# A linear-attention block with an MLP: the output projection of two token blocks by seven block products

## The chip, the cores and the metric

The kernel runs on one core of a Trainium2 chip. The core has a matrix engine (PE; its weight loads are listed as PEld), a vector engine (DVE), a scalar engine (ACT), a general engine (POOL), and a queue that issues transfers (SP). They run side by side and wait for each other through semaphores. PE reads operands from the on-chip memory and writes into eight accumulator banks of 128 x 512 float32; In this kernel DVE and ACT read these banks, and POOL works on the on-chip memory alone. The metric is the time of one execution in microseconds; several executions give a median.

## The reference

The input x has 2048 tokens of 640 features. With xn = layernorm(x), the result is the sum of three parts:

```
q, k, v = split(xn @ wqkv)                 # 32 heads of 20
phi_q, phi_k = [softmax(p), softmax(-p)]   # p = q or k times a 20 x 20 matrix of the head
o = (phi_q (phi_k^T v)) / (phi_q sum(phi_k))
out = x + o @ wo + gelu(layernorm(xn) @ w1 + b1) @ w2 + b2
```

w1 is 640 x 1728, w2 is 1728 x 640, wo is 640 x 640. All is float32.

## The kernel before, in words

**Precision.** The kernel gives PE its operands in the format float32r. It splits each float32 operand exactly into a high part (ACT copies it into float32r) and a low part (DVE or POOL subtracts the high part). A product of two operands is three matmuls, high x high, high x low and low x high; the helper `mm3` (lines 69 to 72) issues them. The helper `split` is at lines 57 to 67: its copy is line 61, its subtraction line 64.

**Tiling.** Tokens stand in four blocks of 512, features in five chunks of 128 (KC = 5). The work of a block is turned: features on the partitions, tokens along the rows. `acc[b]` is the result of block b, five chunks of 128 x 512.

**Order.** The engines PE, DVE, ACT and POOL take their instructions in the order in which the program writes them; SP's order is chosen by the planner from its own estimate of when each transfer can go. The program's clock is the tick: each `mm3` calls `mlp.tick()`, which first runs the steps that are due (`mlp.after(n, step)` puts a step n ticks ahead) and then takes one step of a generator that runs beside (`mlp.beside`).

**Stages.** First the features of block 0, while the MLP begins. The generator `next_y` (from line 653) makes the features of block 1 beside the first two passes of the MLP: POOL subtracts the mean (line 679), DVE multiplies by the inverse deviation (681), ACT makes the high part (683), DVE the low part (685). It also ends what is left of the first block: gelu and split of its hidden units (lines 286 and 64), two tiles of second weights, and the last two instructions of the tokens' statistics, a reciprocal (161) and a product (162) that give `rs_all`, a factor which the attention features use later. Then follow blocks 0 and 1 of the MLP, the projections and the sums of the attention (line 905 and after), the MLP of blocks 2 and 3 beside the attention of all blocks, and the output projection.

**The output projection.** It starts at line 1407. For each block, output chunk m and feature chunk c, one `mm3` multiplies a 128 x 128 piece of wo by the attention output of the block, so that a column (one block and one m) is 15 matmuls into one bank; banks 6 and 7 take turns. DVE adds the bank to `acc[b][:, m]` (line 1423), and SP stores that (1424). The last column goes in two halves of 256 tokens. wo's high and low parts were loaded before (1295, 1297). The attention output of a block is made by `Attention`: `quotients` inverts the denominators (1246, stored by 1247), loads them spread over the partitions into `rx` (1251 to 1256), spreads them further with a shuffle on DVE (1262) and multiplies on POOL (1264). `Attention.split` makes the two parts of the operand, ACT at line 1283 and DVE at 1285, and for blocks 0 and 1 loads the MLP's result back (1289, tf<-a). The split of block 1 starts at tick 3 of the projection, of block 2 at tick 28, of block 3 at tick 53. In the same ticks the `quotients` of block 3 end: its shuffles and products stand at ticks 27 to 42.

The MLP of blocks 2 and 3 already uses, for its first weights, a scheme of seven block products in place of eight (`Mlp.cross`, `Mlp.sums`), with sums of weights made by POOL.

Of the kernel before, what the change touches and what calls it, by code (L numbers as in the profile page):

```python
# [8 lines left out]
F32 = mybir.dt.float32  # L9
F32R = mybir.dt.float32r  # L10
AF = mybir.ActivationFunctionType
ALU = mybir.AluOpType
# [3 lines left out]
P = 128  # L16
S, D, F, H, DH = 2048, 640, 1728, 32, 20
KC = D // P
NB = S // 512
# [27 lines left out]
def f(ap):  # L47
    return ap.bitcast(F32)
# [3 lines left out]
def tile_kernel(ctx: ExitStack, tc: tile.TileContext, x, xT, wkT, wqT, wv, wphi, wo, w1, b1, w2, b2,  # L52
                ident, mmask, emask, vsel, out):
    nc = tc.nc
# [14 lines left out]
    def mm3(ps, lh, ll, rh, rl, first, last, **kw):  # L69
        nc.tensor.matmul(ps, lh, rh, start=first, stop=False, **kw)  # L70
        nc.tensor.matmul(ps, lh, rl, start=False, stop=False, **kw)  # L71
        nc.tensor.matmul(ps, ll, rh, start=False, stop=last, **kw)  # L72
# [25 lines left out]
    acc = [None] * NB  # L98
# [4 lines left out]
    banks = ctx.enter_context(tc.tile_pool(name="banks", bufs=1, space=PSUM))  # L103
# [13 lines left out]
    rp = ys.enter_context(tc.tile_pool(name="raw", bufs=1))  # L117
    wp = ys.enter_context(tc.tile_pool(name="w", bufs=1))

    def mtile(i, dtype=F32):  # L120
        return mp.tile([P, 2, D if i < 5 else 512], dtype, name=f"m{i}")
    y = {}

    def load_x(ts, xp, tag="xb"):
        xbs = []
        for t in ts:
            xb = xp.tile([P, D], F32, name=tag)
            nc.sync.dma_start(xb, x[t * P:(t + 1) * P, :])
            xbs.append(xb)
        return xbs  # L130

    def stats(ts, xp, xbs, turned=False, eng=nc.vector):

        t0, n = ts[0], len(ts)
        st = xp.tile([P, n, 2, 6], F32, name="st", bufs=2)
        for i, (t, xb) in enumerate(zip(ts, xbs)):
            for h in range(2):
                nc.vector.bn_stats(st[:, i, h, :], xb[:, h * 320:(h + 1) * 320])  # L138
            nc.vector.bn_aggr(mv[:, t, :], st[:, i, :, :])
            yield  # L140


        ts = slice(t0, t0 + n)
        q = xp.tile([P, 2, n], F32, name="q", bufs=2)
        eng.tensor_scalar(q[:, 1, :], mv[:, ts, 1], 0.25 * (1 + EPS), 0.25 * EPS * EPS, op0=ALU.mult, op1=ALU.add)
        eng.tensor_scalar(q[:, 0, :], mv[:, ts, 1], 0.25, 0.25 * EPS, op0=ALU.mult, op1=ALU.add)
        yield

        sr = xp.tile([P, 2, n], F32, name="sr", bufs=2)
        rr = xp.tile([P, 2, n], F32, name="rr", bufs=2)  # L150
        nc.scalar.activation(sr, q, AF.Sqrt)
        nc.vector.reciprocal(rr, sr)
        nc.vector.tensor_tensor(rr, rr, q, op=ALU.mult)
        if turned:
            nc.vector.scalar_tensor_tensor(sr, sr, -1.0, rr, op0=ALU.mult, op1=ALU.subtract)
        else:
            nc.vector.tensor_tensor(sr, sr, rr, op=ALU.add)
        nc.vector.reciprocal(ry[:, ts], sr[:, 1, :])
        yield
        ra = xp.tile([P, n], F32, name="ra", bufs=2)  # L160
        nc.vector.reciprocal(ra, sr[:, 0, :])
        nc.vector.tensor_tensor(rs_all[:, ts], sr[:, 1, :], ra, op=ALU.mult)
# [41 lines left out]
    def load_rows(b, i=5):  # L204

        mr = mtile(i)
        loads[b] = nc.sync.dma_start(mr.rearrange("p a t -> p (a t)"),
                          (r_dram[1][0] if b == 1 else r_dram[2][b - 2]).rearrange("r t -> (r t)").unsqueeze(0).to_broadcast([P, 8 * P])).ins
        return mr
# [307 lines left out]
    mlp = Mlp((0, 1, 2, 3), ((0, 2), (1, 3)))  # L517

    def finish(p):
        for _ in p:  # L520
            pass
# [4 lines left out]
    x0 = load_x(range(2), xp)  # L526
    nc.sync.dma_start(idt, ident)
    wc, parts, dmas = {}, {}, {}
# [24 lines left out]
    x1 = load_x(range(4, 8), xp)  # L553
# [99 lines left out]
    def next_y():  # L653

        for _ in range(3):
            yield
        next(rows1)
        for z in zs[:2]:
            z()
        finish(rows1)  # L660
        mr = load_rows(1)
        first_raws.extend(raws(jobs[0]))
        for z in zs[2:]:
            z()
        for c in range(2, 4):
            parts[c][1]()
        for st in (s23, s47):
            step(st, 1)
        for _ in range(4):
            yield  # L670
        nc.vector.tensor_tensor(wpt[:, :, :, 1:], wpt[:, :, :, 1:], wpt[:, :, :, 0:1].to_broadcast([G6, 6, 6, DF]), op=ALU.subtract)
        for _ in range(9):
            yield
        xcs = {}
        for n in range(2 * KC + 5):
            c, i = divmod(n, 2)
            if i == 0 and c < KC:
                xcs[c] = xp.tile([P, D], F32, name="xb")[:, :512]
                nc.gpsimd.tensor_tensor(xcs[c], acc[1][:, c], mr[:, 0], op=ALU.subtract)
            if i == 0 and 0 <= (d := c - 1) < KC:  # L680
                nc.vector.tensor_tensor(xcs[d], xcs[d], mr[:, 1], op=ALU.mult)
            if i == 1 and 0 <= (d := c - 1) < KC:
                nc.scalar.activation(y[1][0][:, d], xcs[d], AF.Copy)
            if i == 0 and 0 <= (d := c - 2) < KC:
                nc.vector.tensor_tensor(y[1][1][:, d], xcs[d], f(y[1][0][:, d]), op=ALU.subtract)
            yield

    mlp.beside = next_y()
    p10 = mlp.passes(1, 0, [wc[2], wc[3]])
    next(p10)  # L690
# [191 lines left out]
    a = ExitStack()  # L882
# [129 lines left out]
    places = [acc01.tile([P, KC, 512], F32, name=f"acc{n}").rearrange("p c (j n) -> p (c j) n", n=P) for n in range(2)]  # L1012
    places = [p[:, j:j + 10] for p in places for j in (0, 10)] + [et.tile([P, 10, P], F32, name="et")]


    for t, i in [(t, i) for t in range(14) for i in range(4)] + TAIL:
        if (t, i) in ((4, 0), (8, 0)):
            b = t // 4 + 1
# [92 lines left out]
    t1 = sp.tile([VM, 5, 480], F32, name="t1")  # L1111
# [198 lines left out]
    wol, phs = [], []  # L1310
    ep = rx = None
# [20 lines left out]
    at = {}  # L1332
# [21 lines left out]
    ep = ctx.enter_context(tc.tile_pool(name="eB", bufs=1, side="right", reuse_waits="tile"))  # L1354
# [14 lines left out]
    for g in range(1, 6):  # L1369
        w2t, later = gathered(g)  # L1370
        hid, more = mlp.cross(g, (2, 3), before, later)
        if g < 5:
            parts = mlp.splits(g + 1)
        else:
            w1t, parts = mlp.take_pair(6, False, 1)
# [14 lines left out]
    w2t, parts = mlp.take_pair(6, True, 3)  # L1390
# [13 lines left out]
    finish(before)  # L1404
    load_ob(1)

    pw_ = Banks(6, 7)
    step = 0
    for b in range(NB):
        oh, ol = at[b].oh, at[b].ol  # L1410
        for m in range(KC):
            ms = slice(m * P, (m + 1) * P)

            for cols in [slice(0, 512)] if (b, m) != (NB - 1, KC - 1) else [slice(0, 256), slice(256, 512)]:
                pw = pw_()[:, cols]
                for c in range(KC):
                    mm3(pw, wol[0][c][:, ms], wol[1][c][:, ms], oh[:, c, cols], ol[:, c, cols], c == 0, c == KC - 1)
                    step += 1
                    mlp.tick()
                    for n, at_ in enumerate((3, 28, 53), 1):  # L1420
                        if step - at_ in range(KC + 1):
                            at[n].split(step - at_, nc.vector)
                nc.vector.tensor_tensor(acc[b][:, m, cols], pw, acc[b][:, m, cols], op=ALU.add)
                nc.sync.dma_start(out[ms, b * 512 + cols.start:b * 512 + cols.stop], acc[b][:, m, cols])


_INS = ["x", "xT", "wkT", "wqT", "wv", "wphi", "wo", "w1", "b1", "w2", "b2", "ident", "mmask", "emask", "vsel"]
# [60 lines left out]
```

## Time and profile before

| | us |
|---|---|
| median of 3 runs | 712.24 (711.95 to 714.44) |
| the profiled execution | 711.95 |
| its span, first to last instruction | 710.2 |
| PE busy | 703.4 |
| DVE busy | 514.5 |
| POOL busy | 421.7 |
| ACT busy | 341.5 |

The mean granted clock of PE is 0.999. In rows of a time line, the first number is the start in us from the span's start, the second the time in us (of all instructions of a row with a count), and what stands in brackets is how long the engine idled before and what ended that. In rows of waits the numbers are us in total, how often, and the longest. In rows of stretches the columns are PE, PEld, DVE, ACT and POOL busy with the count of instructions, the granted clock, the DMA engines' share and GB/s. A row's line can be that of a helper.

### The profile page before, as it was taken

How to read it: one execution, taken by the hardware profiler on the slowest of the kernel's cores; microseconds unless marked ns; L12 is line 12 of the kernel's file. 1: busy time of each engine (PE TensorE's matmuls, PEld its weight loads, DVE VectorE, ACT ScalarE, POOL GpSimd, SP SyncE). 2: the span in 40 equal slices, each digit the busy share in tenths (PEclk: the TensorE clock that was granted, in tenths of full speed). 3: DMA queues.
4: the chain of work that ended last, by engine and by line, in shares of the span. 5: the costliest groups of instructions: out<-in, count | busy, mean ns of one | idle time of the engine just before them, and what ended most of it. 6: DMA issues, size and time to landing. Idle time of an engine off the chain costs nothing.

```text
span 710.2 us, 9748 instructions
## 1 busy us (share of the span) xinstructions
PE 703.4 (99%) x3381; PEld 591.9 (83%) x3381; DVE 514.5 (72%) x819; ACT 341.5 (48%) x563; POOL 421.7 (59%) x362
## 2 busy tenths in 40 slices
PE   9999999999999999999999999999999999999998
PEld 7788888888888888888888888888888878888886
DVE  7977755978754788788888878757769686884622
ACT  6534554344334545544544547367666766450100
POOL 3621314577245997898787879458679887540400
PEclk9999999999999999999999999999999999999999
DMA  9823643485621227336401608963455568436222
GB/s 327 271 90 114 191 119 97 156 264 176 214 105 74 93 75 238 78 105 200 104 0 25 167 0 335 226 209 112 124 163 155 169 188 315 147 125 214 86 78 74
DMA packets 65767, 106.56 MB, mean 150 GB/s; under 512 B 7462, under 2 KB 31814, under 8 KB 63838
## 3 DMA queue, kind: packets, MB, share of 16 engines
q1 hardware_dynamic: 65414, 105.93, 46.7%
q8 instruction: 26, 0.43, 0.3%
q14 instruction: 23, 0.19, 0.1%
q10 hardware_dynamic: 304, 0.01, 0.0%
HBM read 71.37 MB, written 34.55 MB: 149 GB/s over the span
## 4 chain that ended last, share of the span: by engine, by line
PE 94%; DVE 3%; DMA 1%; ACT 1%; issue 0%; SPq 0%; DVEq 0%
PE bank L905 28%; PE bank L70 19%; PE bank L72 18%; PE bank L71 18%; PE bank L975 3%; PE bank L646 2%; PE bank L1213 1%; PE bank L1214 1%; DMA xb<-in_x 1%; DVE st L138 1%; DMA r<-sr 1%; PE bank L326 1%; PE bank L308 1%; PE bank L327 1%; PE bank L307 1%; PE bank L1145 1%
## 5 line engine op out<-in xcount | busy, mean ns | idle before, releaser
L905 PE MATMUL bank<-wkh,y 128*128 128x512 f32 (+1 forms) x480 | 139.5, 364 | 0.0
L70 PE MATMUL bank<-y,w 128*128 128x512 f32 (+1 forms) x294 | 114.3, 389 | 0.0
L71 PE MATMUL bank<-y,w 128*128 128x512 f32 (+1 forms) x294 | 113.7, 387 | 0.0
L72 PE MATMUL bank<-y,w 128*128 128x512 f32 (+1 forms) x294 | 113.6, 387 | 0.0
L64 POOL TENSOR_TENSOR w<-r,w 128x640 fp32r<-128x640 f32 x32 | 52.2, 1647 | 91.7 <-ACT w L61 62.2
L70 PE MATMUL bank<-m,w 128*128 128x512 f32 x260 | 102.4, 394 | 1.2 <-DVE acc L329 1.0
L72 PE MATMUL bank<-m,w 128*128 128x512 f32 x260 | 101.3, 390 | 0.0
L71 PE MATMUL bank<-m,w 128*128 128x512 f32 x260 | 101.2, 389 | 0.0
L905 PEld LDWEIGHTS bank<-wkh,y 128*128 128x128 f32 x480 | 87.5, 188 | 13.3
L905 PE MATMUL bank<-wkl,y 128*128 128x512 f32 (+1 forms) x240 | 87.4, 364 | 0.0
L70 PEld LDWEIGHTS bank<-y,w 128*128 128x128 f32 x294 | 55.2, 188 | 11.6 <-issue 0.4
L72 PEld LDWEIGHTS bank<-y,w 128*128 128x128 f32 x294 | 55.2, 188 | 11.3
L71 PEld LDWEIGHTS bank<-y,w 128*128 128x128 f32 x294 | 55.3, 188 | 11.0
L941 ACT ACTIVATE m<-m,rs_all 128x1280 f32<-128x1280 f32 x32 | 43.7, 1366 | 42.9 <-POOL m L940 42.8
L70 PEld LDWEIGHTS bank<-m,w 128*128 128x128 f32 x260 | 48.9, 188 | 12.1 <-DVE acc L329 1.5
L943 DVE TENSOR_REDUCE sm<-m 128x64 f32<-128x1280 f32 x32 | 47.4, 1482 | 14.9 <-ACT m L941 14.8
L905 PE MATMUL bank<-w,y 128*128 128x512 f32 x240 | 57.4, 391 | 0.0
L72 PEld LDWEIGHTS bank<-m,w 128*128 128x128 f32 x260 | 48.8, 188 | 10.3
L71 PEld LDWEIGHTS bank<-m,w 128*128 128x128 f32 x260 | 48.8, 188 | 9.9 <-DVE m L461 0.2
L940 POOL TENSOR_TENSOR m<-m,mx 128x640 f32<-128x640 f32 (+2 forms) x48 | 44.4, 938 | 19.3 <-DVE mx L929 19.3
L331 DVE TENSOR_TENSOR acc<-bank,acc 128x512 f32<-128x512 f32 x70 | 46.9, 683 | 10.9 <-PE bank L72 5.8
L905 PEld LDWEIGHTS bank<-w,y 128*128 128x128 f32 x240 | 44.4, 188 | 8.5
(186 smaller groups left out, 1447.2 us busy)
## 6 DMA issues: line engine op xcount, KB each, us to landing
r<-in_w SPq DMA_DIRECT2D x52, 320.0 KB
e<-e SPq DMA_DIRECT2D x40, 256.0 KB
e<-acc SPq DMA_DIRECT2D x52, 160.0 KB
acc<-in_xT SPq DMA_DIRECT2D x4, 1280.0 KB
t<-t SPq DMA_DIRECT2D x8, 512.0 KB
tf<-t SPq DMA_DIRECT2D x2, 1536.0 KB
xb<-in_x SPq DMA_DIRECT2D x8, 320.0 KB
t<-in_x SPq DMA_DIRECT2D x8, 320.0 KB
```

The costliest lines, as they stand in the source:

```text
L64: eng.tensor_tensor(lo, src, f(hi), op=ALU.subtract)
L70: nc.tensor.matmul(ps, lh, rh, start=first, stop=False, **kw)
L71: nc.tensor.matmul(ps, lh, rl, start=False, stop=False, **kw)
L72: nc.tensor.matmul(ps, ll, rh, start=False, stop=last, **kw)
L138: nc.vector.bn_stats(st[:, i, h, :], xb[:, h * 320:(h + 1) * 320])
L331: nc.vector.tensor_tensor(acc[b][:, m, :], pw, acc[b][:, m, :], op=ALU.add)
L646: nc.tensor.matmul(ps[:, u * nh * DF:(u + 1) * nh * DF], raw[:nh * DH, u * P:(u + 1) * P], wpt[:nh * DH, g, :nh, 1:], start=True, stop=True)
L905: nc.tensor.matmul(ps, lh[:, kc, c], rh[:, kc], start=n == 0, stop=n == 3 * KC - 1)
L940: subs[n, t] = nc.gpsimd.tensor_tensor(ep[:, s], a, b, op=ALU.subtract)
L941: exps[n, t] = nc.scalar.activation(e, e, AF.Exp, scale=rs_all[:, t:t + 1])
L943: nc.vector.tensor_reduce(sm, e.rearrange("p s (h f) -> p (s h) f", f=DH), axis=AX, op=ALU.add)
L975: nc.tensor.matmul(kvp[g // 2][:, (g % 2) * 240:(g % 2) * 240 + 240].rearrange("p (s f) -> p s f", s=4), v[:, g * VS:(g + 1) * VS], ft[:, ...
```

## The change

**Output projection.** Blocks 0 and 1 stay as they were, now by the function `column`. For blocks 2 and 3, four of the five output chunks and four of the five feature chunks are multiplied as 2 x 2 blocks of matrices with seven products in place of eight: with a_ij from wo and b_ij from the features (j is the token block, i the feature chunk in a pair), four sums s1 to s4 of wo and four differences t1 to t4 of the features are made first. The products run for k = 0, 1 (pairs of output chunks) and q = 0, 1 (pairs of feature chunks); a product's bank is read by DVE between two products, and goes on accumulating. The fifth feature chunk is added by `rest`, the fifth output chunk is a `column`. The sums of wo come from a new load of 512 x 512 numbers (`load_sums`, into the slot w3, which held the last second weights of the MLP); POOL adds (`add`), ACT makes the high parts into slot w1 (`hi_sum`), DVE the low parts into the slots of `kvs` and `s` (`lo_sum`). For the differences POOL subtracts (`combine`), ACT copies the result twice, once as the high part and once into bank 3 or 4 (`turn_hi`), and DVE subtracts the high part from that bank (`turn_lo`). All of these are steps at fixed ticks. The split of block 3 moves from tick 53 to 59.

**Start.** The last two instructions of the statistics of tiles 2 and 3 and of tiles 4 to 7 (lines 161 and 162) move in `next_y` from ahead of block 1's features to behind them.

```
@@ next_y @@
         for c in range(2, 4):
             parts[c][1]()
-        for st in (s23, s47):
-            step(st, 1)
         for _ in range(4):
             yield
...
                 nc.vector.tensor_tensor(y[1][1][:, d], xcs[d], f(y[1][0][:, d]), op=ALU.subtract)
+            yield
+        for st in (s23, s47):
+            step(st, 1)
             yield
@@ output projection @@
+    def load_sums():
+        sums.append(wp.tile([P, 4, D], F32, name="w3").rearrange("p i d -> p (i d)")[:, :4 * 512])
+        nc.sync.dma_start(sums[0].rearrange("p (c n) -> p c n", c=4), wo[:4 * P, :512].rearrange("(c p) n -> p c n", p=P))
...
+    def add(i):
+        (a11, a12), (a21, a22) = ([sums[0].rearrange("p (q r k j n) -> p q r k j n", q=2, r=2, k=2, j=2)[:, :, r, :, j] for r in range(2)] for j in range(2))
+        o, x0, x1, op = ((a22, a21, a22, ALU.add), (a21, a11, a21, ALU.subtract), (a11, a22, a11, ALU.subtract), (a12, a12, a11, ALU.subtract))[i]
+        nc.gpsimd.tensor_tensor(o, x0, x1, op=op)
+    def hi_sum(c):
+        nc.scalar.activation(sums[1][:, c * 512:c * 512 + 512], sums[0][:, c * 512:c * 512 + 512], AF.Copy)
+    def lo_sum(o, w):
+        at_ = slice(o, o + w)
+        nc.vector.tensor_tensor(lo_part(o)[:, :w], sums[0][:, at_], f(sums[1][:, at_]), op=ALU.subtract)
+    def combine(i, q):
...
+        o = ep.tile([P, 512], F32, name="e", bufs=6) if i in (2, 3) else x[2, c0 if i == 1 else c1]
+        x0, x1 = {1: lambda: (x[3, c0], x[2, c0]), 2: lambda: (x[3, c1], t[1]), 3: lambda: (x[3, c1], x[3, c0]), 4: lambda: (x[2, c1], t[2])}[i]()
+        nc.gpsimd.tensor_tensor(o, x0, x1, op=ALU.subtract)
+    def turn_hi(i, q):
...
+        bank = copies()
+        for o in (parts[0], bank):
+            nc.scalar.activation(o.rearrange("p (t q n) -> p t q n", q=4, t=4), src, AF.Copy)
+    def turn_lo(i, q):
+        _, bank, (hi, lo) = turned[i, q]
+        nc.vector.tensor_tensor(lo, bank, f(hi), op=ALU.subtract)
+    steps = [(1, load_sums)]
+    steps += [(12 + 2 * i, lambda i=i: add(i)) for i in range(4)]
+    steps += [(20 + c, lambda c=c: hi_sum(c)) for c in range(4)]
+    steps += [(22 + n, lambda o=o, w=w: lo_sum(o, w)) for n, (o, w) in enumerate(((0, 512), (512, 512), (1024, 256), (1280, 256), (1536, 512)))]
+    for n, (i, q) in enumerate((i, q) for i in (1, 2, 4, 3) for q in range(2)):
+        steps += [(42 + 2 * n, lambda i=i, q=q: combine(i, q)), (45 + 2 * n, lambda i=i, q=q: turn_hi(i, q)), (46 + 2 * n, lambda i=i, q=q: turn_lo(i, q))]
+    for n, t in ((1, 3), (2, 28), (3, 59)):
+        steps += [(t + c, lambda n=n, c=c: at[n].split(c, nc.vector)) for c in range(KC + 1)]
...
+    for b in range(2):
         for m in range(KC):
...
+            column(b, m, [6 + (b + m) % 2])
...
+    def product(n, k, l, r, start=False):
+        for q in range(2):
+            mm3(places[n, k], left(l, 0, q, k), left(l, 1, q, k), *right(r, q), start and q == 0, q == 1, skip_group_check=True)
+            mlp.tick()
...
+    def read(n, k, i, b, last=True):
+        m = 2 * k + i
+        nc.vector.tensor_tensor(acc[b][:, m], places[n, k], acc[b][:, m], op=ALU.add)
+        if last:
+            nc.sync.dma_start(out[m * P:(m + 1) * P, b * 512:(b + 1) * 512], acc[b][:, m])
+    for k in range(2):
+        place("a", k, k)
+        product("a", k, "a11", "b11", True)
+        read("a", k, 0, 2, False)
+        place("c", k, (2, 5)[k])
+        product("c", k, "a12", "b21", True)
+        rest("c", k, 0, 2)
+        read("c", k, 0, 2)
+    column(2, 4, [2])
+    for k in range(2):
+        place("b", k, (5, 2)[k])
+        product("b", k, "s1", "t1", True)
+        read("b", k, 1, 3, False)
+        product("a", k, "s2", "t2")
+        read("a", k, 0, 3, False)
+        place("c", k, (2, 5)[k])
+        product("c", k, "a22", "t4", True)
+        rest("c", k, 1, 2)
+        read("c", k, 1, 2, False)
+        product("a", k, "s3", "t3")
+        read("a", k, 1, 2)
+        product("b", k, "s4", "b22")
+        rest("b", k, 0, 3)
+        read("b", k, 0, 3)
+        rest("a", k, 1, 3)
+        read("a", k, 1, 3)
+    column(3, 4, [0, 5], (slice(0, 256), slice(256, 512)))
```

More of the change, by code (lines that the diff above doesn't have):

```diff
@@ L1405, in tile_kernel @@
     load_ob(1)
[L1407 to L1410, printed above, removed]
-        for m in range(KC):
[L1412 to L1424, printed above, removed]
+    sums, turned = [], {}
@@ new lines, in load_sums @@
+    def load_sums():
+        sums.append(wp.tile([P, 4, D], F32, name="w3").rearrange("p i d -> p (i d)")[:, :4 * 512])
+        nc.sync.dma_start(sums[0].rearrange("p (c n) -> p c n", c=4), wo[:4 * P, :512].rearrange("(c p) n -> p c n", p=P))
+        hi = wp.tile([P, 4, D], F32R, name="w1").rearrange("p i d -> p (i d)")
+        lo = [bp.tile([P, 11, P], F32R, name="kvs").rearrange("p i d -> p (i d)"), rp.tile([P, 3, 2, P], F32R, name="s").rearrange("p i k n -> p (i k n)")]
+        sums.extend([hi, lo])
@@ new lines, in lo_part @@
+    def lo_part(o):
+        return sums[2][0][:, o:] if o < 5 * 256 else sums[2][1][:, o - 5 * 256:]
+    def add(i):
[4 more added lines that the diff above has]
+        nc.scalar.activation(sums[1][:, c * 512:c * 512 + 512], sums[0][:, c * 512:c * 512 + 512], AF.Copy)
@@ new lines, in lo_sum @@
+    def lo_sum(o, w):
+        at_ = slice(o, o + w)
+        nc.vector.tensor_tensor(lo_part(o)[:, :w], sums[0][:, at_], f(sums[1][:, at_]), op=ALU.subtract)
+    def combine(i, q):
+        c0, c1 = 2 * q, 2 * q + 1
+        x = {(b, c): at[b].ob[:, c] for b in (2, 3) for c in (c0, c1)}
+        t = {j: turned[j, q][0] for j in (1, 2, 3, 4) if (j, q) in turned}
+        o = ep.tile([P, 512], F32, name="e", bufs=6) if i in (2, 3) else x[2, c0 if i == 1 else c1]
+        x0, x1 = {1: lambda: (x[3, c0], x[2, c0]), 2: lambda: (x[3, c1], t[1]), 3: lambda: (x[3, c1], x[3, c0]), 4: lambda: (x[2, c1], t[2])}[i]()
+        nc.gpsimd.tensor_tensor(o, x0, x1, op=ALU.subtract)
+        turned[i, q] = [o]
@@ new lines, in tile_kernel @@
+    copies = Banks(3, 4)
+    def turn_hi(i, q):
+        src = turned[i, q][0].rearrange("p (q t n) -> p t q n", q=4, t=4)
+        n = 2 * (i - 1) + q
+        if n == 7:
+            parts = [ep.tile([P, 512], F32, name="e", bufs=6).bitcast(F32R) for _ in range(2)]
+        else:
+            m = mtile(n, F32R)
+            parts = [m[:, p, :512] for p in range(2)]
+        bank = copies()
+        for o in (parts[0], bank):
+            nc.scalar.activation(o.rearrange("p (t q n) -> p t q n", q=4, t=4), src, AF.Copy)
+        turned[i, q] += [bank, parts]
@@ new lines, in tile_kernel, with column @@
+    for n, t in ((1, 3), (2, 28), (3, 59)):
+        steps += [(t + c, lambda n=n, c=c: at[n].split(c, nc.vector)) for c in range(KC + 1)]
+    for t, step in sorted(steps, key=lambda e: e[0]):
+        mlp.after(t, step)
+    def column(b, m, banks_of, parts=(slice(0, 512),)):
+        ms = slice(m * P, (m + 1) * P)
+        for n, cols in zip(banks_of, parts):
+            pw = banks.tile([P, 512], F32, name=f"bank{n}")[:, cols]
+            for c in range(KC):
+                mm3(pw, wol[0][c][:, ms], wol[1][c][:, ms], at[b].oh[:, c, cols], at[b].ol[:, c, cols], c == 0, c == KC - 1)
+                mlp.tick()
+            nc.vector.tensor_tensor(acc[b][:, m, cols], pw, acc[b][:, m, cols], op=ALU.add)
+            nc.sync.dma_start(out[ms, b * 512 + cols.start:b * 512 + cols.stop], acc[b][:, m, cols])
@@ new lines, in tile_kernel, with place, left @@
+    for b in range(2):
+        for m in range(KC):
+            column(b, m, [6 + (b + m) % 2])
+    places = {}
+    def place(n, k, i):
+        places[n, k] = banks.tile([P, 512], F32, name=f"bank{i}")
+    def left(n, p, q, k):
+        i, j = {"a11": (0, 0), "a12": (1, 0), "a22": (1, 1), "s1": (1, 1), "s2": (0, 0), "s3": (0, 1), "s4": (1, 0)}[n]
+        c, o = 2 * q + i, (2 * k + j) * P
+        if n[0] == "a":
+            return wol[p][c][:, o:o + P]
+        return sums[1][:, c * 512 + o:c * 512 + o + P] if p == 0 else lo_part(c * 512 + o)[:, :P]
@@ new lines, in right, with rest @@
+    def right(n, q):
+        if n[0] == "t":
+            return turned[int(n[1]), q][2]
+        i, j = int(n[1]) - 1, int(n[2]) - 1
+        return [z[:, 2 * q + i] for z in (at[2 + j].oh, at[2 + j].ol)]
+    def product(n, k, l, r, start=False):
+        for q in range(2):
+            mm3(places[n, k], left(l, 0, q, k), left(l, 1, q, k), *right(r, q), start and q == 0, q == 1, skip_group_check=True)
+            mlp.tick()
+    def rest(n, k, i, b):
+        ms = slice((2 * k + i) * P, (2 * k + i + 1) * P)
+        mm3(places[n, k], wol[0][4][:, ms], wol[1][4][:, ms], at[b].oh[:, 4], at[b].ol[:, 4], False, True, skip_group_check=True)
+        mlp.tick()
```

## The prediction

> **What bounds the kernel now.** I read the page's first part, then TensorE's waits, then time lines of the two places that the change touches: the start and the output projection.
>
> ```profile
> span 710.2 us, 9748 instructions
> PE 703.4 (99%) x3381; PEld 591.9 (83%) x3381; DVE 514.5 (72%) x819; ACT 341.5 (48%) x563; POOL 421.7 (59%) x362
> ```
>
> ```profile
> PE bank L579 <- POOL m L577: 1.3, 1, 1.3
> PE bank L70 <- DVE acc L329: 1.0, 1, 1.0
> PE bank L1213 <- DVE acc L1227: 0.6, 1, 0.6
> PE bank L70 <- ACT w L61: 0.2, 1, 0.2
> ```
>
> TensorE is busy for 703.4 of 710.2 us and waits 3.1 us in all, so time is won only by fewer matmuls or by one of these waits. What a matmul costs is read from the output projection (PE: its first matmul; DVE: evictions of columns).
>
> ```profile
> 638.26 0.47 PE L70 MATMUL bank<-y,w 128*128 128x512 f32 x1
> ...
> 643.32 0.69 DVE L1423 TENSOR_TENSOR tf<-bank,tf 128x512 f32<-128x512 f32 x1 [1.96 <-DMA tf<-a]
> 652.18 0.69 DVE L1423 TENSOR_TENSOR tf<-bank,tf 128x512 f32<-128x512 f32 x1 [2.71 <-PE bank L72]
> 655.58 0.69 DVE L1423 TENSOR_TENSOR tf<-bank,tf 128x512 f32<-128x512 f32 x1 [2.71 <-PE bank L72]
> 659.14 0.68 DVE L1423 TENSOR_TENSOR tf<-bank,tf 128x512 f32<-128x512 f32 x1
> 692.98 0.69 DVE L1423 TENSOR_TENSOR acc<-bank,acc 128x512 f32<-128x512 f32 x1 [2.71 <-PE bank L72]
> 696.38 0.69 DVE L1423 TENSOR_TENSOR acc<-bank,acc 128x512 f32<-128x512 f32 x1 [2.71 <-PE bank L72]
> 706.77 0.42 DVE L1423 TENSOR_TENSOR acc<-bank,acc 128x256 f32<-128x256 f32 x1 [1.37 <-PE bank L72]
> ```
>
> A column is 15 matmuls and takes 696.38 - 692.98 = 3.40 us, so a matmul costs 0.227 us, although a group's mean of one is near 390 ns (they overlap). A tick, three matmuls, is 0.68 us; tick n ends at 638.26 + 0.68n.
>
> **The matmuls removed.** Blocks 2 and 3 now take 2 x 5 x 5 x 3 = 150 matmuls (the last column in halves counted whole). After: 7 products x 2 (k) x 2 (q) x 3 = 84, the fifth chunk 8 x 3 = 24, two columns of output chunk 4 at 15 each = 30; together 138. 12 x 0.227 = 2.72 us goes if nothing new waits. The end keeps its form: a column in halves, its eviction, its store.
>
> **The first edit, at the start.** Two reciprocals and two products move behind block 1's features. These are DVE's, POOL's, ACT's and PE's rows around them.
>
> ```profile
> 19.34 0.16 DVE L162 TENSOR_TENSOR rs_all<-sr,ra 128x2 f32<-128x2 f32 x1
> 25.95 1.33 DVE L162 TENSOR_TENSOR rs_all<-sr,ra 128x2 f32<-128x2 f32 x1
> 27.41 1.41 DVE L162 TENSOR_TENSOR rs_all<-sr,ra 128x4 f32<-128x4 f32 x1
> 28.74 0.68 DVE L64 TENSOR_TENSOR m<-m,m 128x512 fp32r<-128x512 f32 x1
> 38.79 1.17 DVE L681 TENSOR_TENSOR xb<-xb,m 128x512 f32<-128x512 f32 x1
> 48.09 0.69 DVE L64 TENSOR_TENSOR m<-m,m 128x512 fp32r<-128x512 f32 x1 [2.13 <-ACT m L61]
> ```
>
> ```profile
> 25.64 3.15 POOL L64 TENSOR_TENSOR w<-r,w 128x640 fp32r<-128x640 f32 x2 [0.75 <-ACT w L61]
> 31.76 7.65 POOL L679 TENSOR_TENSOR xb<-acc,m 128x512 f32<-128x512 f32 x5 [2.96 <-DMA m<-r]
> ```
>
> ```profile
> 26.80 0.63 ACT L61 ACTIVATE m<-m 128x512 fp32r<-128x512 f32 x1
> ```
>
> ```profile
> 31.51 0.50 PE L70 MATMUL bank<-m,w 128*128 128x512 f32 x1 [1.04 <-DVE acc L329]
> ```
>
> The products take 1.33 and 1.41 us where the same one took 0.16, and the second ends (28.82) with POOL's pair (25.64 + 3.15 = 28.79): they stand waiting for POOL. Behind them come L64, the weights' subtraction, L64 and then the L329 for which PE waits 1.04 us, so up to 1.04 us could go. But the L64 that comes next has its operand at 26.80 + 0.63 = 27.43, while POOL still works; it reads two operands outside the accumulator banks, like L681 at 38.79, which ended at 39.96, 0.55 after POOL's 31.76 + 7.65 = 39.41. So L64 would end at 28.79 + 0.55 = 29.34 and not at 29.42: a gain of 0.1. I take 0.1 of the span 0 to 1.04, since that row shows the same kind of instruction in the same place. At their new place the four instructions stand before the L64 at 48.09, where DVE idles 2.13 us waiting for ACT; even held up by POOL they took 28.82 - 25.95 = 2.87 from the first product on, and an L64 0.7 late has the rest of a pass of PE in front of its use: nothing, 0.3 at most.
>
> The Trainium skill (SBUF — State Buffer, Who interferes with whom) says that of a GpSimd instruction and a VectorE instruction with two SBUF inputs the later one blocks fully until the first ends. By that rule the first edit is worth 0.1 and the time 709.4; without it, 1.04 and 708.5. The rows above agree with it.
>
> **The sums of wo.** One load of 1 MB by SP at tick 1 into the slot w3, which is free once the last pass's matmuls end (638.3), then four POOL sums, four ACT copies, five DVE subtractions. SP's queue and the transfers there:
>
> ```profile
> 637.59 0.32 SPq L1289 DMA_DIRECT2D tf<-a  x1
> 640.24 0.33 SPq L1247 DMA_DIRECT2D d<-dt  x1
> 643.45 0.50 SPq L1251 DMA_DIRECT2D rx<-d  x1
> 645.84 0.32 SPq L1289 DMA_DIRECT2D tf<-a  x1
> 647.16 0.52 SPq L1256 DMA_DIRECT2D rx<-d  x1
> ```
>
> ```profile
> 641.00:642.00 1.00, 1.00 (x6) 0.82 (x5) 0.35 (x1) 0.00 (x0) 0.00 (x0) 1.00 0.98 389
> 642.00:643.00 1.00, 1.00 (x6) 0.83 (x5) 0.00 (x0) 0.00 (x0) 0.00 (x0) 1.00 0.52 188
> 643.00:644.00 1.00, 1.00 (x6) 0.84 (x5) 0.68 (x2) 0.00 (x0) 0.00 (x0) 1.00 0.00 1
> 655.00:656.00 1.00, 1.00 (x6) 0.84 (x5) 0.42 (x1) 0.37 (x1) 0.00 (x0) 1.00 0.00 0
> ```
>
> (The last two columns are the DMA engines' share and GB/s.) The 64 KB d<-dt is issued at 640.24, but rx<-d, which waits for it, goes only at 643.45, when the 1.3 MB of tf<-a before it (5 x 512 numbers in each of 128 partitions) are through: the queue serves in order. 1.05 MB at 389 GB/s is 2.7 us. If the load goes behind tf<-a, the first eviction is as before; d<-dt and everything that SP has behind it (five rx<-d, the second tf<-a, three stores) moves by 2.7 us, the last rx<-d to 649.9. All these transfers were done by 655.0, stores included, so now by 657.7 at the latest. The second tf<-a is wanted at 659.14. The rx are wanted by the shuffle:
>
> ```profile
> 656.20 0.75 DVE L1262 STREAM_SHUFFLE rx<-rx 128x512 f32<-128x512 f32 x1
> ...
> 673.30 1.29 DVE L1285 TENSOR_TENSOR y<-acc,y 128x512 fp32r<-128x512 f32 x2
> ```
>
> ```profile
> 655.63 2.72 ACT L1283 ACTIVATE y<-acc 128x512 fp32r<-128x512 f32 x5 [20.50 <-PE bank L72]
> ```
>
> ```profile
> 657.03 3.34 POOL L1264 TENSOR_TENSOR acc<-acc,rx 128x512 f32<-128x512 f32 x2 [24.30 <-DVE rx L1262]
> 664.10 2.54 POOL L1264 TENSOR_TENSOR acc<-acc,rx 128x512 f32<-128x512 f32 x2 [0.20 <-DVE rx L1262]
> ```
>
> At worst the shuffle is 1.5 us late and the eviction at 659.14 with it, done at 661.3; PE wants its bank at tick 35, 662.1. Cost 0. The sums: landed near 643.32 + 2.7 = 646.0, POOL (idle for 24.30 us) 4 x 1.3 = 5.2 to 651.2, ACT (idle for 20.50) 0.54 each to 652.9, DVE 4 x 0.65 = 2.6 from tick 22 (653.2), in gaps of 2.71 us between evictions. PE first uses them at tick 65, 682.5. What stands behind DVE's subtractions is the eviction at 655.58; PE wants its bank at tick 30, 658.7, so they may slip by 2.3 us. With the load landing at L, the fourth subtraction ends near L + 7.0 and the eviction at L + 7.7: no stall up to L = 651.0.
>
> **The differences of the features.** POOL has eight, ACT sixteen copies, DVE eight subtractions, ticks 42 to 60. POOL's first comes behind the fourth product of block 3 (664.10 + 1.27 = 665.4); nine instructions (one product among them) of 1.27 to 1.3 end at 677.1, ACT's two copies 1.1 later, DVE's subtraction at 678.9. It is issued at tick 60, 679.1. With POOL's slow 3.34 / 2 = 1.67 it is 682.2, the eviction behind it 682.9, and bank 5, wanted at tick 65 (682.5), costs 0.5. I take 0, as these subtractions read a bank and one other operand, and the eviction at 659.14 of that kind took 0.68 beside a busy POOL.
>
> **DVE's evictions** go from 11 to 19, 8 x 0.69 = 5.5 us on an engine that idles 2.71 of 3.40 us there. The tightest return is bank a between s2 x t2 and s3 x t3: three ticks, 2.04 us, for one eviction of 0.69 plus some 0.3 (651.86 to 652.18) before it. No wait. Block 3's split, moved from tick 53 to 59, ends at tick 64; b22 is wanted at tick 74.
>
> **Sum.** 2.72 + 0.1 = 2.8 us off. The profiled execution took 711.95 (span 710.2 and 1.75 around it), 0.29 under the median 712.24; against the median 709.4. 0.5%, 3.56 us, is about what a measurement of this kernel can tell from no change (runs of before lie 711.95 to 714.44); the gain stays under it.
>
> **Rivals.** (1) The load of sums stands before tf<-a in SP's queue. Their issues would lie only 0.7 us apart (637.59 and 638.3), and SP's order is planned, not written. tf<-a landed 643.32 - 637.59 = 5.73 us after its issue; behind the load that is 638.3 + 2.7 + 5.73 = 646.7, the first eviction ends at 647.4, and PE, which wants that bank at tick 10 (645.1), stands 2.4 us with the way to PE: 711.8. Against it: tf<-a is the earlier of the two in the code, and it could go before the slot was free.
>
> (2) The other side: the load comes late, behind the last rx<-d and the second tf<-a. The second tf<-a lands at 645.84 + 5.73 = 651.6, the load 2.7 later at 654.3; DVE's subtractions hold the eviction of tick 25 to 662.0, PE stands 3.4 us, and the shuffles and POOL's products follow late: 712.8 and up, to 716 if the block's later evictions queue too. It decides from L = 651.0 + 2.8 = 653.8. For it: the order is the planner's, and it placed the code's later rx<-d before the second tf<-a. Against: the slot is free at 638.3 and SP issues nothing from 637.91 to 640.24.
>
> (3) The start gives its whole 1.04: 708.5, which needs L64 not to wait for POOL.
>
> (4) The products don't flow: operands a little late, 0.5 to 2 us given back, 710 to 711.3. For it: 0.2 us between 678.9 and 679.1.
>
> **Chances.** Forecast 0.55 (709.4, its own range 708.7 to 710.1), rival 1 0.15, rival 2 0.10, rival 3 0.10, rival 4 0.10. Faster by over 0.5% (under 708.7) is rival 3, 0.10; slower (over 715.8) is the far end of rival 2 and what I don't see, 0.07; the rest 0.83. The range 708.2 to 713.2 takes in rivals 1, 3, 4 and the near end of 2.
>
> **What would show it.** PE's last stretch, from its first matmul of line 70 on tiles y and w to the last eviction, shortens from 68.5 to 65.8 us with no new row among PE's waits; the wait for L329 stays near 1.0; tf<-a is issued before the load of w3; POOL's fourth sum ends before 653. Wrong would be: a wait of PE on the evictions of blocks 0 or 1, a first eviction after 645, or DVE waiting for ACT between 653 and 660.

## The result, and the profile after

The changed kernel takes 709.83 us in the median of 7 runs (709.17 to 710.54), beside 712.92 us before (7 runs, the three shown above among them). The ratio is 0.9955, with a 95% interval of 0.9940 to 0.9969: 3.2 us less, 2.2 to 4.3. Forecast was 2.8 us less. Run again beside the last experiments, the same kernel gave 0.9949 (0.9936 to 0.9961).

The head of the page of the kernel after, and all of PE's waits in it (us in total, times, longest):

```profile
span 708.0 us, 9794 instructions
PE 701.1 (99%) x3369; PEld 590.3 (83%) x3369; DVE 526.4 (74%) x840; ACT 353.1 (50%) x583; POOL 435.6 (62%) x374
```

```profile
PE bank L579 <- POOL m L577: 1.3, 1, 1.3
PE bank L70 <- DVE acc L329: 1.0, 1, 1.0
PE bank L1214 <- DVE acc L1228: 0.6, 1, 0.6
PE bank L70 <- ACT m L449: 0.3, 1, 0.3
PE bank L70 <- ACT w L61: 0.2, 1, 0.2
```

PE has 3369 matmuls instead of 3381, twelve less. DVE has 12 us more work, ACT 12 and POOL 14, and PE's waits hold none on the output projection's lines. The wait for L329, which the first edit stands next to, is still 1.0 us.

The projection's first matmul and last eviction, from the time line of the kernel after:

```profile
638.88 0.47 PE L70 MATMUL bank<-y,w 128*128 128x512 f32 x1
...
704.64 0.42 DVE L1481 TENSOR_TENSOR acc<-bank,acc 128x256 f32<-128x256 f32 x1 [1.37 <-PE bank L72]
```

From the one to the other 704.64 - 638.88 = 65.76 us, before 706.77 - 638.26 = 68.51: 2.75 us less in this stage alone. The two profiled spans differ by only 2.2, since in this execution PE came to the projection 0.62 us later than in that of before. That place varies between executions of one code: the kernel after, profiled again, came to it at 639.99, and `tail_only`, whose code up to there is that of before, at 640.85 where before came at 638.26.

The start: L329 in the kernel before, then POOL's pair and DVE's rows in the kernel after.

```profile
30.72 2.05 DVE L329 SCALAR_TENSOR_TENSOR acc<-bank,b2t,acc 128x512 f32<-128x512 f32 x3
```

```profile
25.63 3.16 POOL L64 TENSOR_TENSOR w<-r,w 128x640 fp32r<-128x640 f32 x2 [0.75 <-ACT w L61]
27.45 1.89 DVE L64 TENSOR_TENSOR m<-m,m 128x512 fp32r<-128x512 f32 x1 [1.62 <-ACT m L61]
29.27 0.86 DVE L669 TENSOR_TENSOR wpt<-wpt 120x684 f32<-120x684 f32 x1
30.05 0.68 DVE L64 TENSOR_TENSOR m<-m,m 128x512 fp32r<-128x512 f32 x1
30.65 2.05 DVE L329 SCALAR_TENSOR_TENSOR acc<-bank,b2t,acc 128x512 f32<-128x512 f32 x3
```

DVE now idles 1.62 us until ACT has made the operand, and then L64 takes 1.89 us instead of 0.68, to 29.34, 0.55 after POOL's pair (28.79). L329 starts at 30.65 instead of 30.72.

The projection: SP's queue, the first eviction, the sums, the shuffle and the end of the differences.

```profile
638.21 0.32 SPq L1290 DMA_DIRECT2D tf<-a  x1
638.95 0.39 SPq L1412 DMA_DIRECT2D w<-in_wo  x1
641.47 0.33 SPq L1248 DMA_DIRECT2D d<-dt  x1
649.41 0.51 SPq L1257 DMA_DIRECT2D rx<-d  x1
```

```profile
643.75 0.69 DVE L1481 TENSOR_TENSOR tf<-bank,tf 128x512 f32<-128x512 f32 x1 [1.77 <-DMA tf<-a]
656.17 0.69 DVE L1481 TENSOR_TENSOR tf<-bank,tf 128x512 f32<-128x512 f32 x1 [0.84 <-PE bank L72]
657.39 0.74 DVE L1263 STREAM_SHUFFLE rx<-rx 128x512 f32<-128x512 f32 x1
660.95 0.67 DVE L1481 TENSOR_TENSOR tf<-bank,tf 128x512 f32<-128x512 f32 x1
679.92 0.69 DVE L1461 TENSOR_TENSOR m<-bank,m 128x512 fp32r<-128x512 f32 x1 [0.56 <-ACT bank L1456]
681.15 0.68 DVE L1518 TENSOR_TENSOR acc<-bank,acc 128x512 f32<-128x512 f32 x1
```

```profile
646.64 5.39 POOL L1424 TENSOR_TENSOR w<-w 128x512 f32<-128x512 f32 x4 [12.90 <-DMA w<-in_wo]
664.91 2.55 POOL L1265 TENSOR_TENSOR acc<-acc,rx 128x512 f32<-128x512 f32 x2 [2.49 <-DVE rx L1263]
667.41 1.29 POOL L1440 TENSOR_TENSOR acc<-acc,acc 128x512 f32<-128x512 f32 x1
673.66 2.57 POOL L1440 TENSOR_TENSOR acc<-acc,e 128x512 f32<-128x512 f32 x2
```

tf<-a goes first, the load of wo (the row of L1412) 0.74 us behind it; the first eviction comes at 643.75, 4.87 after PE's first matmul (5.06 before). POOL's sums run from 646.64 to 652.03, and the eviction of tick 25 at 656.17, behind four of the low parts, is on time.

### The profile page after: what moved, and what is told of

The parts are those of the page before. It is cut to its first block, busy times and chain, and to the rows that moved or that the text cites. A ratio compares the mean times of both kernels' runs of the same rounds, so it can differ in the third digit from the quotient of the medians.

```text
span 708.0 us, 9794 instructions
## 1 busy us (share of the span) xinstructions
PE 701.1 (99%) x3369; PEld 590.3 (83%) x3369; DVE 526.4 (74%) x840; ACT 353.1 (50%) x583; POOL 435.6 (62%) x374
## 4 chain that ended last, share of the span: by engine, by line
PE 93%; DVE 4%; ACT 1%; DMA 1%; issue 0%; ACTq 0%; DVEq 0%; SPq 0%
PE bank L906 28%; PE bank L70 18%; PE bank L72 18%; PE bank L71 18%; PE bank L976 3%; PE bank L646 2%; PE bank L1214 1%; PE bank L1215 1%; DVE st L138 1%; DMA e<-e 1%; PE bank L308 1%; PE bank L327 1%; PE bank L326 1%; PE bank L307 1%; PE bank L1146 1%
## 5 line engine op out<-in xcount | busy, mean ns | idle before, releaser
L64 POOL TENSOR_TENSOR w<-r,w 128x640 fp32r<-128x640 f32 x32 | 52.3, 1648 | 93.1 <-ACT w L61 57.7
L70 PE MATMUL bank<-m,w 128*128 128x512 f32 x274 | 108.0, 394 | 1.1 <-DVE acc L329 1.0
L71 PE MATMUL bank<-m,w 128*128 128x512 f32 x274 | 106.8, 390 | 0.0
L70 PE MATMUL bank<-y,w 128*128 128x512 f32 (+1 forms) x274 | 106.5, 389 | 0.0
L71 PE MATMUL bank<-y,w 128*128 128x512 f32 (+1 forms) x274 | 106.1, 387 | 0.0
L72 PE MATMUL bank<-y,w 128*128 128x512 f32 (+1 forms) x270 | 104.4, 387 | 0.0
L72 PE MATMUL bank<-m,w 128*128 128x512 f32 x262 | 102.1, 390 | 0.0
L70 PEld LDWEIGHTS bank<-m,w 128*128 128x128 f32 x274 | 51.5, 188 | 12.4 <-DVE acc L329 1.4
L70 PEld LDWEIGHTS bank<-y,w 128*128 128x128 f32 x274 | 51.5, 188 | 10.8 <-issue 0.4
L71 PEld LDWEIGHTS bank<-y,w 128*128 128x128 f32 x274 | 51.5, 188 | 10.5 <-DMA y<-t 0.4
L71 PEld LDWEIGHTS bank<-m,w 128*128 128x128 f32 x274 | 51.5, 188 | 10.4 <-DVE m L461 0.2
L72 PEld LDWEIGHTS bank<-y,w 128*128 128x128 f32 x270 | 50.8, 188 | 10.3
L72 PEld LDWEIGHTS bank<-m,w 128*128 128x128 f32 x262 | 49.2, 188 | 10.3
L331 DVE TENSOR_TENSOR acc<-bank,acc 128x512 f32<-128x512 f32 x70 | 47.0, 684 | 11.0 <-PE bank L72 6.1
L64 DVE TENSOR_TENSOR m<-m,m 128x512 fp32r<-128x512 f32 (+1 forms) x34 | 27.9, 828 | 36.0 <-ACT m L61 36.0
```

Of the source, the lines that this page charges most:

```text
L64: eng.tensor_tensor(lo, src, f(hi), op=ALU.subtract)
L331: nc.vector.tensor_tensor(acc[b][:, m, :], pw, acc[b][:, m, :], op=ALU.add)
```

## The experiments

Ratios are to the kernel before; 0.001 is 0.71 us. "Stretch" is PE's first matmul of the projection to the start of the last eviction, 68.51 us before and 65.76 after.

**1. The first edit alone, and the products alone** (`start_only`, `tail_only`). This edit of the kernel before; and the same edit taken back in the kernel after:

```
             parts[c][1]()
-        for st in (s23, s47):
-            step(st, 1)
...
             yield
+        for st in (s23, s47):
+            step(st, 1)
+            yield
```

> The kernel before with the first edit alone (the last statistics of tiles 2 to 7 behind block 1's features). Theory: POOL's subtraction, 27.23 to 28.79, holds DVE's next L64 instead, so PE's wait for L329 stays at 1.0 us and the time is that of before within 0.3 us. Rival (the start gives its whole wait): PE's wait for L329 is gone and the time falls by 1.0 us.

> The kernel after without the first edit, so the seven products alone. Theory: 12 matmuls of 0.227 us are gone and nothing new waits: 2.7 us under before, PE's stretch from the projection's first matmul to the last eviction's start 68.5 to 65.8 us. Rival (the products give some back): the same stretch 66.3 us or more and PE waits in it.

The first edit alone gives 0.9998 (0.9988 to 1.0008), with a wait of 0.9 us for L329. The products alone give 0.9961 (0.9947 to 0.9975), with a stretch of 706.64 - 640.85 = 65.79 us. So the products alone give 2.8 of the 3.2 us, and the start alone 0.1, which 12 runs can't tell from nothing.

**2. Half of the products** (`half`).

```
-    for k in range(2):
+    for k in range(1):
         place("a", k, k)
...
-    column(2, 4, [2])
-    for k in range(2):
+    for m in (2, 3, 4):
+        column(2, m, [6 + m % 2])
+    for k in range(1):
...
+    for m in (2, 3):
+        column(3, m, [6 + m % 2])
     column(3, 4, [0, 5], (slice(0, 256), slice(256, 512)))
```

> The kernel after with the seven products for k = 0 alone; output chunks 2 and 3 of blocks 2 and 3 are columns, as before. Six matmuls more than after: theory 6 x 0.227 = 1.36 us over after, 1.4 under before. Rival (the gain is not in the count of matmuls but in the order or in the start): as after, or as before.

0.9980 (0.9969 to 0.9990), that is 1.4 us under before; stretch 706.95 - 639.79 = 67.16 us, where 68.51 - 6 x 0.227 = 67.15. The gain goes with the count of matmuls.

**3. The side work** (`no_side`).

```
-    steps = [(1, load_sums)]
-    steps += [(12 + 2 * i, lambda i=i: add(i)) for i in range(4)]
...
+    steps = []
...
-        if n[0] == "a":
+        if n:
             return wol[p][c][:, o:o + P]
...
+        i, j = (0, 1) if n[0] == "t" else (int(n[1]) - 1, int(n[2]) - 1)
```

> The kernel after without the sums of wo and the differences of the features (no load of wo, no work of POOL, ACT and DVE for them): the seven products take plain pieces of wo and plain features in their place, so blocks 2 and 3 of the output are not the reference's. Theory: all that work is hidden, the time is that of after within 0.3 us. Rival (it takes part of the gain): 0.5 us or more under after.

0.9962 (0.9949 to 0.9974), stretch 65.79 us: without the load, the sums and the differences the kernel is no faster. POOL is busy 15.2 us less than in after, ACT 10.9 and DVE 6.2: some 32 us of work on three engines is hidden whole.

**4. Where the load of wo stands in SP's queue** (`load_first`, `load_late`, and later `load_half_first`).

In load_first tf<-a of block 0 is issued behind the load, whose instruction is `ld`; in load_late the load is issued at tick 15, behind the last rx<-d of block 3, and the four sums stand at ticks 16 to 19.

```
@@ load_first, in load_sums @@
+        with tc.issue_after(ld):
+            nc.sync.dma_start(acc[0], a_dram[0])
@@ load_late, at tick 15 @@
+        with tc.issue_after(last_rx[-1]):
+            nc.sync.dma_start(sums[0].rearrange("p (c n) -> p c n", c=4), wo[:4 * P, :512].rearrange("(c p) n -> p c n", p=P))
```

> The kernel after with SP's queue forced: the load of wo for the sums goes ahead of tf<-a of block 0. Theory: the queue serves in order, so tf<-a lands 2.7 us later and besides goes out 0.7 to 1.1 us later; the first eviction moves from 643.8 to near 647, PE waits 2 to 3 us for it, and the time is 2 to 3 us over after, near before. Rival (both transfers share the engines, or the bank has more slack): under 1 us over after.

> The kernel after with the load of wo for the sums behind the last rx<-d of block 3 in SP's queue. Theory: it lands near 654, DVE's low parts of the sums hold the eviction of tick 25 until about 662, and PE waits some 3 us for it: 3 us over after, equal to before or over it. Rival (the sums are wanted at 682 only and nothing stands behind them): as after.

load_first: 1.0011 (0.9999 to 1.0023), which is 4.0 us over after: the whole gain is gone for the order of two neighbours in a queue. load_late: 1.0075 (1.0062 to 1.0089), 8.6 us over after. Both directions were right and both sizes too small. In load_first, the first eviction, PE's row at the wait, two rows a little later, and stretches of 1 us (the last three columns: clock, DMA share, GB/s):

```profile
647.74 0.69 DVE L1484 TENSOR_TENSOR tf<-bank,tf 128x512 f32<-128x512 f32 x1 [5.47 <-DMA tf<-a]
648.49 0.50 PE L70 MATMUL bank<-y,w 128*128 128x512 f32 x1 [2.27 <-DVE tf L1484]
650.25 0.63 PE L70 MATMUL bank<-y,w 128*128 128x512 f32 x1
650.67 0.63 PE L71 MATMUL bank<-y,w 128*128 128x512 f32 x1
```

```profile
648.00:649.00 1.00, 0.51 (x2) 0.47 (x3) 1.00 (x2) 0.33 (x1) 0.92 (x2) 1.00 0.00 0
650.00:651.00 1.00, 1.00 (x4) 0.81 (x3) 1.00 (x2) 0.64 (x2) 0.33 (x1) 0.50 0.19 70
652.00:653.00 1.00, 1.00 (x4) 0.81 (x3) 0.08 (x1) 0.04 (x1) 0.00 (x0) 0.50 0.94 170
653.00:654.00 1.00, 1.00 (x6) 0.83 (x5) 0.18 (x1) 0.00 (x0) 0.00 (x0) 0.97 0.75 266
```

The wait of 2.27 us is what the queue's order predicted (2.4). But from 649.7 to 653.1, for 3.4 us, the granted clock is 0.50 and matmuls start 650.67 - 650.25 = 0.42 us apart instead of 0.23: half of 3.4, 1.7 us more, and 2.27 + 1.7 = 4.0; this execution's stretch is 709.12 - 639.17 = 69.95 us, 4.19 over after. The fall did not come every time. Of the twelve executions, eight have a mean granted clock of 0.997 or 0.998 over the whole kernel and took 713.06 to 716.28 us; the other four have 1.000 and took 712.01 to 713.54. The median of these four is 712.26, some 2.4 to 2.8 over after: there the wait cost about its length.

In load_late the load landed at 658.3, later than the 654 I had reckoned, and POOL's sums, the eviction and PE's wait are

```profile
658.30 5.32 POOL L1427 TENSOR_TENSOR w<-w 128x512 f32<-128x512 f32 x4 [24.04 <-DMA w<-in_wo]
665.60 0.68 DVE L1484 TENSOR_TENSOR tf<-bank,tf 128x512 f32<-128x512 f32 x1
666.34 0.79 PE L70 MATMUL bank<-y,w 128*128 128x512 f32 x1 [5.87 <-DVE tf L1484]
```

with the clock at half for 6.8 us, of which PE worked through 3.6: 5.87 + 1.8 = 7.7 of the 8.6 us. All six executions have a mean clock of 0.994 or 0.995. The eviction that it waited for started at 665.60, behind the fourth low part, as supposed; it ended 8.0 us after the load had landed, where I had reckoned 7.7. So the low parts of the sums, wanted only at tick 65, can hold PE at tick 30 already.

To see whether the clock falls after any wait there, half of the load went first (`to` and `of` are the load's target and source):

```
+        ld = nc.sync.dma_start(to[:, :2], of[:, :2]).ins
+        with tc.issue_after(ld):
+            ld = nc.sync.dma_start(acc[0], a_dram[0]).ins
+        with tc.issue_after(ld):
+            nc.sync.dma_start(to[:, 2:], of[:, 2:])
```

> As the run with the load of wo ahead of tf<-a, but only half of it (chunks 0 and 1, 0.5 MB) goes ahead, the other half behind tf<-a. In that run PE waited 2.3 us, and for some 3 us after it PE's granted clock was down (0.69 over 650 to 655) and matmuls came every 0.43 us. Theory: half the bytes ahead, tf<-a lands 1.35 us earlier than there, PE waits about 1 us, its clock stays up as after its other waits of 1 us, and the time is 1 to 1.5 us over after instead of 4. Rival (the clock falls after any wait at this place): 2.5 us or more over after.

```profile
648.12 0.50 PE L70 MATMUL bank<-y,w 128*128 128x512 f32 x1 [0.94 <-DVE tf L1487]
```

```profile
650.00:655.00 5.00, 5.00 (x24) 3.96 (x23) 2.27 (x3) 0.72 (x2) 4.65 (x4) 1.00 0.68 199
```

PE waits 0.94 us and its clock stays at 1.00; the mean clock is 0.999 or 1.000 in all eleven executions. The time is 0.9974 (0.9965 to 0.9983), 1.4 to 1.8 us over the two measurements of after. The stretch is 707.24 - 640.13 = 67.11 us, 1.35 over after: 0.4 more than the listed wait, but without the half clock. The first eviction comes 7.25 us after PE's first matmul, where it was 8.57 with the whole load ahead and 4.87 in after; half of the load is worth 1.32 us of that.

**5. The copy into a bank** (`two_memory`).

```
-        for o in (parts[0], bank):
+        for o in (parts[0],):
...
-        nc.vector.tensor_tensor(lo, bank, f(hi), op=ALU.subtract)
...
+        nc.vector.tensor_tensor(lo, src, f(hi), op=ALU.subtract)
```

`src` is the difference itself, in the memory that POOL works on.

> The kernel after without ACT's second copy into a bank: DVE's low parts of the differences read the difference itself, so both their operands stand in the memory that POOL works on. Theory: each of the eight then waits for POOL's current subtraction and takes over 1 us instead of 0.69, POOL's slow down too, and evictions queue behind them; bank 5, wanted at 682.5, comes late and PE waits 0 to 2 us. Rival (the copy into the bank buys nothing): eight at 0.7 us and the time as after.

0.9976 (0.9967 to 0.9986), 1.5 us over after. One of DVE's low parts, the eviction that PE then waits for, and PE's rows at the two places where it is held:

```profile
675.65 1.18 DVE L1463 TENSOR_TENSOR m<-e,m 128x512 fp32r<-128x512 f32 x1
683.29 0.68 DVE L1520 TENSOR_TENSOR acc<-bank,acc 128x512 f32<-128x512 f32 x1
...
684.12 0.47 PE L70 MATMUL bank<-m,w 128*128 128x512 f32 x1 [0.80 <-ACT y L1284]
...
686.70 0.39 PE L72 MATMUL bank<-m,kvs 128*128 128x512 f32 x1
687.13 0.47 PE L70 MATMUL bank<-m,w 128*128 128x512 f32 x1
```

```profile
674.54 3.44 POOL L1440 TENSOR_TENSOR acc<-acc,e 128x512 f32<-128x512 f32 x2
```

Each of the low parts beside a busy POOL takes 1.18 to 1.55 us instead of 0.69, and POOL's pairs 3.44 instead of 2.57; the last low part, at 682.08 when POOL has ended, takes 0.69. DVE falls behind, and PE waits 0.80 us at tick 65, where the bank is wanted. The profile names ACT, which had begun that work at 681.96 for a matmul further on; the eviction that ends at 683.97 fits the wait better. At 687.13 a matmul starts 0.43 us after the one before it instead of 0.23, again behind an eviction. The stretch is 705.97 - 638.84 = 67.13 us, 1.37 over after, nearly all of the 1.5.

**6. Taking POOL out of the way at the start** (`start_free`, `start_one`, `start_one_dve`). If POOL's subtraction is what holds L64, moving it must end the wait for L329.

start_free moves the second weights of tiles 2 and 3, start_one those of tile 3 alone, and start_one_dve is start_one with three subtractions of the mean on DVE:

```
@@ start_free @@
-        for c in range(2, 4):
-            parts[c][1]()
         for _ in range(4):
...
-        for _ in range(9):
+        for _ in range(3):
+            yield
+        for c in range(2, 4):
+            parts[c][1]()
+        for _ in range(6):
             yield
@@ start_one_dve @@
-                nc.gpsimd.tensor_tensor(xcs[c], acc[1][:, c], mr[:, 0], op=ALU.subtract)
+                (nc.gpsimd if c < 2 else nc.vector).tensor_tensor(xcs[c], acc[1][:, c], mr[:, 0], op=ALU.subtract)
```

> The kernel after, with the copies and POOL's subtractions of the second weights of tiles 2 and 3 three ticks behind the subtraction of line 669, so that POOL is idle when DVE's L64 comes. Theory: that L64 takes 0.7 us instead of 1.9, PE's wait for L329 (1.0 us) goes and the time falls by 0.7 to 1.0 us below the kernel after; what could take it back is block 1's features, which come 0.6 us ahead of their use. Rival (the wait has another cause than POOL, the eviction being late of itself): the wait and the time stay.

> The kernel after, with the copy and POOL's subtraction of the second weights of tile 3 alone three ticks behind the subtraction of line 669. Moving both took PE's wait for L329 away, but POOL's subtractions of the mean came 1.6 us later and PE waited 0.8 us for an eviction of line 331 instead. Theory: POOL now works from 25.6 to 27.3 and again from 29.2, DVE's two L64 take 0.7 us each, the subtractions of the mean start near 30.8 as in the kernel after; PE's wait for L329 goes, but DVE's work on block 1's features still ends near 45, so a part of the 1.0 us comes back as waits for L331 or the features: 0 to 0.7 us under after. Rival (the wait moves whole, since DVE's queue there is full): as after.

> As the run before it, with the last three subtractions of the mean on DVE instead of POOL. DVE gets 3 x 0.6 us more work and loses the waits for POOL (0.6, 0.4 and 1.1 us in the kernel after). Theory: DVE's stretch ends about as in the kernel after or 0.3 us earlier and the order in its queue lets evictions go sooner: 0.3 to 1.0 us under after. Rival (the queue is only longer): 0 to 1 us over after.

start_free, some of DVE's rows, and the waits of PE for these two evictions:

```profile
27.32 0.69 DVE L64 TENSOR_TENSOR m<-m,m 128x512 fp32r<-128x512 f32 x1 [1.48 <-ACT m L61]
29.31 2.06 DVE L329 SCALAR_TENSOR_TENSOR acc<-bank,b2t,acc 128x512 f32<-128x512 f32 x3
37.02 1.77 DVE L685 TENSOR_TENSOR y<-xb,y 128x512 fp32r<-128x512 f32 x1
38.72 0.68 DVE L331 TENSOR_TENSOR acc<-bank,acc 128x512 f32<-128x512 f32 x1
```

```profile
PE bank L70 <- DVE acc L331: 1.0, 2, 0.8
PE bank L70 <- DVE acc L329: 0.2, 1, 0.2
```

L64 takes 0.69 us, L329 starts 1.34 earlier, and PE's wait for it is gone (the 0.2 that is left stands at 36.12, for a later eviction of that line): POOL was the cause. But 0.9961 (0.9947 to 0.9974) is no faster than after. A wait of 0.8 us for L331 stands in its place, an eviction behind L685, which takes 1.77 us beside POOL's subtraction of the mean.

The moved weights are not the only way to that wait: load_half_first, whose start is that of after, has it too. POOL's subtraction of the mean began at 30.70 in after; in start_free and in load_half_first it began later:

```profile
32.33 7.60 POOL L679 TENSOR_TENSOR xb<-acc,m 128x512 f32<-128x512 f32 x5
```

```profile
33.08 7.61 POOL L677 TENSOR_TENSOR xb<-acc,m 128x512 f32<-128x512 f32 x5 [4.34 <-PE bank L72]
40.22 0.50 PE L70 MATMUL bank<-m,w 128*128 128x512 f32 x1 [0.79 <-DVE acc L331]
```

What made it late in load_half_first is not shown. start_one gives 0.9936 (0.9923 to 0.9948) and start_one_dve 0.9933 (0.9919 to 0.9947), beside 0.9949 of after in the same set of runs: 0.9 and 1.1 us less, a little more than expected, with intervals that overlap. In both the wait for L329 is gone and one for L331 is left, of 0.8 and 0.6. These two are the fastest seen, and lie under both kernels; that they beat the kernel after is likely, not certain.

## Why the prediction was right

**The matmuls removed** were the gain. 12 x 0.227 = 2.72 us was the forecast, 2.75 the stage's difference, and half of them gave half. The 0.227, from one matmul's start to the next, came from columns in the trace; the mean of one matmul in the page's groups, near 390 ns, would have given 4.7.

**The start**, 0.1 of up to 1.04 us: L64 ended at 29.34 as reckoned, L329 moved by 0.07, and the edit alone measured nothing. This also bears out the rule of the Trainium skill on the shared port (SBUF — State Buffer, Who interferes with whom), by which the one that comes second is blocked until the first ends, with 1.89 us for the L64 that came second. Rival 3 is out. What the prediction did not see is the next wait behind this one: start_free ended that for L329 and had one for L331 in DVE's queue, so the 1.04 us was no measure of what freeing L64 alone would give.

**The sums.** tf<-a stood first, by 0.74 us, so rival 1 did not happen; load_first shows what it would have cost. The load landed at 646.6 (646.0 reckoned), the last rx<-d went at 649.41 (649.9), the shuffle ran at 657.39 (by 657.7), the eviction behind it ended at 661.6 (661.3). No wait of PE.

**The differences.** The last low part ended at 680.6; with this execution's projection starting 0.62 later, 679.5 was reckoned. POOL's pace was as reckoned (2.57 us a pair), but its first difference started at 667.41 and not at 665.4 + 0.62 = 666.0, as POOL's products wait for DVE's shuffles, and these ran later, behind the low parts of the sums and then of block 2's features. That is a wait which the prediction allowed for the evictions and not for POOL. The eviction behind ended at 681.8; the bank was wanted at 638.88 + 65 x 0.68 = 683.1. Rival 4 did not happen, with 1.3 us to spare. That these subtractions, with one operand in a bank, don't wait for POOL was argued from one row, and two_memory shows it: 0.69 against 1.18 to 1.55 with both operands in the memory, and 0.69 there too once POOL has ended.

**DVE's eight more evictions** cost nothing, as reckoned.

**What failed** is the price in the rivals. Both priced a wait of PE by its length (2.4 us and 3.4 us); load_first and load_late show 4.0 and 8.6. The mechanisms, the queue's order and the eviction behind the low parts, were those described, but the terms left out the clock. In load_first the price of 2.4 holds for the four executions whose clock stayed up, and not for the other eight. In load_late the load landed 658.30 - 639.79 = 18.5 us after PE's first matmul, where rival 2 had 654.3 - 638.26 = 16.0; these 2.5 us more and the 3.4 make up the wait of 5.87, and the clock came on top. load_late is slower than before by more than 0.5%, which had a chance of 0.07; what the load would cost where rival 2 put it no run shows.

**Luck.** The forecast time, 709.4, was counted from a median of before, 712.24, that was low: 7 runs gave 712.92 and later sets 713.12 to 713.38. The measured gain, 3.2 us (3.6 in the second measurement), is larger than the stage's 2.75, which lies within the first interval; no run shows where the rest comes from, if it is there.

## What to carry to other kernels

Cost removed matmuls at their spacing in a full stretch, not at the mean of one, and then ask of each piece of side work which queue it stands in and who is behind it: the sums were wanted 24 us after the place where they could first have stopped PE. A wait of PE can cost more than its length: here that of load_first, 2.27 us in the profiled execution, did in eight of twelve, through the clock. And when a wait is traced to a blocked engine, look for the next wait behind it before counting its length as gain.

## What the runs showed of the hardware

- The granted clock fell to 0.50 after waits of PE of 2.27 us (for 3.4 us) and 5.87 us (for 6.8 us), and not after waits of 0.94 us at the first of these places or 1.04 us at the start. By the mean clock, the fall came in eight of the twelve executions of load_first and in all six of load_late. The Trainium skill (TensorE: Matmul & The Clock Gate, Part 1) has a half clock after an idle window of some 3.4 us, and the same page of the Trainium skill (Why this matters for your kernels) advises against idle gaps of over some 3 us; here 2.27 us sufficed, so the measurement decides. The length of 3.4 us, and twice that, agrees with its window.
- An instruction of DVE with both operands in the memory that POOL works on ended 0.55 us after POOL's (29.34 after 28.79); with one operand in a bank it took 0.69 us beside a busy POOL.
- One queue's transfers ran in order: with 1 MB ahead of tf<-a the first eviction waited until 647.74, where it was 643.75. Of this, tf<-a's own issue was 1.5 us later (639.72 instead of 638.21); with half of that load moved behind it, the first eviction came 1.32 us sooner, counted from PE's first matmul.
